# First queries and keys by two plain transfers each, values requested before the placing, the second pair's rounding one step later

## The chip, the cores and the metric

The kernel runs on one core of one Trainium2 chip. The core has five engines with an instruction queue each: TensorE (PE; its weight loads are shown as PEld), VectorE (DVE), ScalarE (ACT), GpSimd (POOL) and SyncE (SP), which here issues every DMA. Sixteen DMA engines carry the transfers. The metric is the device time of one execution in microseconds (us); of a kernel the median of its runs is given.

## What is computed

Attention that keeps, for every query, the scores that reach the 32nd largest, then two feed-forward blocks. Cut to what matters (B, H, S, D = 4, 8, 576, 64):

```
scores = scale * q @ k.T                      # per batch and head, 576 x 576
kth = 32nd largest of each row
attn = softmax(where(scores >= kth, scores, -1e9)) @ v
x = attn of all heads, side by side           # 2304 x 512
x = soft mixture of 8 experts on 32 slots (phi, w1, w2)
out = (g of x @ w_in) @ w_out                 # g(h) = h * tanh(softplus(h))
```

## The kernel before

Attention comes first. Heads are taken in 16 pairs (four batches of four). The 1152 queries of a pair are nine tiles of 128; two tiles make a step, so attention has 72 steps, numbered m. Steps -2 and -1 only produce scores. Within `run` (L415) the list `ORDER` fixes by hand in which order the pieces of a step are written, and every engine executes its own instructions in that order.

One step of one pair of tiles goes like this. TensorE makes scores (L223) from operands that are kept as sums of a rounded and a low part: `Qs` holds rounded queries above their low parts, `Ka` the rounded keys twice, `Kb` the low parts of the keys and the row of maxima. ScalarE copies the scores, four copies of 288 columns a step, into a tile `x` (L433). VectorE folds `x` (h L238, f L239 and L240) and finds the 32nd largest value by rounds of eight maxima (L260, L264, L267); GpSimd adds two operations to the fold (f L246, L250). In step -1 VectorE does GpSimd's part (L242). Then ScalarE makes a mask `R` (L280) and exponentials (L321), and TensorE multiplies with the values (L326). Scores and copies are made two steps ahead of the maxima, the fold one step ahead. The tile h has one buffer.

Loading has three layers. Pair i needs queries and keys with the heads on 128 partitions (`load`, L153, into `rawq` and `rawk`, one buffer each), their rounding on ScalarE (`split_hi`, L158), the low parts (`split_lo`, L161: VectorE for pair 0, GpSimd for the others), and copies inside SBUF which put the parts of each head into `Qs`, `Ka` and `Kb` (`place`, L173, five transfers a head, and `place_b`, L176). `load_v` (L191) brings `vT` and the values `V` in five transfers; `phi` comes in two.

The very first head has a way of its own, `first_head` (L178): it loads 64 rows of queries and 64 rows of keys, each onto both halves of the partitions, into a tile `E`, rounds them on ScalarE straight into place (L185, L186), and VectorE writes the rest (L187 to L189). No placing is needed. The second head of pair 0 goes by `load` and `place`. Twelve matmuls on zeros (L147) warm TensorE up meanwhile.

For the later pairs `prepare` (L569) puts each of these pieces at a step, `LEAD` steps from the pair's first; the function `at` (L427) moves what would be due earlier to step -1, or to -2 for loads. Only pair 1 (first step 4) is touched by that limit: its roundings and the low part of its queries were put at step -1, and the placing of its first head.

Weight fetches for the experts are written between the steps of attention. Experts and the last block follow.

Of the kernel before, what the change touches and what calls it, by code (L numbers as in the profile page):

```python
# [23 lines left out]
B, H, S, D = 4, 8, 576, 64  # L24
# [65 lines left out]
class Attention:  # L90
# [87 lines left out]
    def first_head(self):  # L178

        nc = self.nc  # L180
        raw = self.w2.tile([128, 2, 576], F32, name="E")
        for n, name in enumerate("qk"):
            nc.sync.dma_start(raw[:, n], self.io[name + "T"][0, 0, None, 0:64].to_broadcast([2, 64, 576]))
        hi = self.w2.tile([128, 576], F32R, name="V")
        nc.scalar.copy(hi, raw[:, 0])  # L185
        nc.scalar.copy(self.Ka[0], raw[:, 1])  # L186
        nc.vector.tensor_copy(self.Qs[0][0:64, :576], hi[0:64].bitcast(F32))  # L187
        nc.vector.tensor_tensor(self.Qs[0][64:128, :576], raw[64:128, 0], hi[64:128].bitcast(F32), op=ALU.subtract)
        nc.vector.tensor_tensor(self.Kb[0][0:64], raw[0:64, 1], self.Ka[0][0:64].bitcast(F32), op=ALU.subtract)  # L189
# [225 lines left out]
    def run(self, between=None):  # L415
        nc = self.nc
# [5 lines left out]
        todo, carry, sides = collections.defaultdict(list), {}, dict(x=([], []), y=([], []))  # L422
# [2 lines left out]
                ended[n // 2] = i, GROUPS[t]  # L425

        def at(m, token, f):  # L427
            todo[max(m, -2 if token == "Z" else -1)].append((token, f))

        def copy(m, ps, u, hf):  # L430
            if m not in X:
# [39 lines left out]
        def side(name, m, engine):  # L471

            wait, now = sides[name]
            if not now and wait and wait[0][0] <= m:
                g = wait.pop(0)[1]
                now += [g, next(g)]
            if now and engine in (now[1], None):
                now[1] = next(now[0], "")
                if not now[1]:
                    now.clear()  # L480

        def step(m):
# [39 lines left out]
            if m - 2 in ended:  # L522

                iv, gv = ended[m - 2]
                for slot in IN_GROUP[gv[4]]:
                    add("v", lambda slot=slot: values(exs[m - 2][0], iv, gv, slot))
                if gv[1][-1] in (4, 8):

                    key, rs, rc = (iv, gv[0]), [], []
                    at(m + 1, "s", lambda: rs.append(self.sums(avs[key], key[1], m > M)))  # L530
                    at(m + 1, "i", lambda: rc.append(self.recip(rs[0])))
                    if m > M:
                        at(m + 1, "i", lambda: self.last_logits(avs[key], rc[0], iv))
                    for t in range(5):
                        at(m + 1, "n", lambda t=t: self.normalize(avs[key], rc[0], xls[key[0]], key[1], t))
                    at(m + 2, "l", lambda: ending(*key))
# [32 lines left out]
        def prepare(j):  # L569

            first = 9 * j // 2
            d = Ds[j] = {}
            for n in "qk":
                at(first + LEAD[0], "Z", lambda n=n: self.load(d, j, n))
            for q, n in enumerate("qk"):
                at(first + LEAD[1] + q, "H", lambda n=n: self.split_hi(d, n))
                at(first + LEAD[2] + q, "L", lambda n=n: self.split_lo(d, n, nc.gpsimd))
            for h in range(2):
                for n in "qk":
                    at(first + LEAD[3] + h, "D", lambda h=h, n=n: self.place(d, j, h, n))  # L580
            at(first + LEAD[4], "D", lambda: self.load_v(d, j))
            for h in range(2):
                at(first + LEAD[6 + h], "D", lambda h=h: self.place_b(j, h))
            sides["y"][0].append((first + LEAD[5], self.fold_phi(d, j)))

        with self.tc.manual_schedule(engines={ENG.Activation, ENG.PE, ENG.DVE, ENG.Pool, ENG.SP}):
            d = Ds[0] = {}
            self.first_head()
            for n in "qk":
                self.load(d, 0, n)  # L590
            for n in "qk":
                self.split_hi(d, n)
                self.split_lo(d, n, nc.vector)
                self.place(d, 0, 1, n)
            pv = self.io["phi"].rearrange("(p h d) s -> h d p s", h=2, d=D)
            for h in range(2):
                nc.sync.dma_start(self.phi[64 * h : 64 * h + 64, :, 32 * h : 32 * h + 32], pv[h])
            self.load_v(d, 0)
            sides["y"][0].append((0, self.fold_phi(d, 0)))
            for h in range(2):  # L600
                self.place_b(0, h)
            for j in range(1, npairs):
                prepare(j)
            for m in range(-2, M + 4):
                step(m)
            n = iter(IDLE)

            def warm():
                for _ in range(next(n)):
                    nc.tensor.matmul(idle[:, :256], self.k.idn.bitcast(BF16)[:, :128], self.k.idn.bitcast(BF16), start=True, stop=True)  # L610

            while sum(sides["x"], []):
                if sides["x"][1] and sides["x"][1][1] == "P":
                    warm()
                side("x", M, None)
            warm()
# [439 lines left out]
```

## Time and profile before

| | us |
|---|---|
| median of 3 runs | 855.86 |
| the runs | 850.24 to 857.74 |
| the profiled execution | 856.29 |
| its span, from the first to the last instruction | 854.4 |
| TensorE busy | 762.4 (89%) |
| VectorE busy | 742.8 (87%) |
| ScalarE busy | 592.0 (69%) |
| GpSimd busy | 414.5 (49%) |
| mean granted TensorE clock | 0.953 of full speed |

All times in rows are microseconds from the span's start. A row of a timeline gives the start, the length, the engine, the line, the operation, what is written and read, and in brackets how long the engine had been idle and what ended that. SPq is the queue of SyncE; its rows give how long the issue of a transfer took, not the transfer. A clock of 1.00 is the full 2.4 GHz, 0.50 the lower level, 1.2 GHz.

### The profile page before, as it was taken

The numbers are of one execution on the slowest core, as the hardware profiler recorded it, in microseconds if no ns is written. First come the engines' busy times: TensorE is split into PE (matmuls) and PEld (weight loads), VectorE is DVE, ScalarE is ACT, GpSimd is POOL, SyncE is SP. The second block draws the span as 40 slices with busy tenths as digits, with TensorE's granted clock in tenths as the row PEclk, the third lists the DMA queues.
The fourth block names the chain that finished last, engine by engine and source line by source line (L and its number), as shares of the span: only waits on it lengthen the run. The fifth ranks groups of instructions, "written<-read, shape, count | busy, mean of one in ns | idle before, by whom it ended". The sixth has DMA issues, their size and how long they took to land.

```text
span 854.4 us, 17813 instructions
## 1 busy us (share of the span) xinstructions
PE 762.4 (89%) x6222; PEld 657.3 (77%) x6222; DVE 742.8 (87%) x2206; ACT 592.0 (69%) x1330; POOL 414.5 (49%) x475
## 2 busy tenths in 40 slices
PE   4689999999999999999999998885378889999997
PEld 2578898898888899888988886653366677888885
DVE  3999999997997999999999936869989999869673
ACT  3478888886887888989888743328664755766462
POOL 3466576565665556666665610003444544443332
PEclk7699999998998999999999999996789999999999
DMA  3636545643653755465344478990220001001011
GB/s 83 162 78 168 127 122 151 169 116 95 168 135 86 208 130 152 119 168 126 70 106 126 157 289 330 399 371 9 90 99 0 1 37 38 1 0 74 1 38 42
DMA packets 60984, 103.41 MB, mean 121 GB/s; under 512 B 24852, under 2 KB 24852, under 8 KB 59860
## 3 DMA queue, kind: packets, MB, share of 16 engines
q1 hardware_dynamic: 60884, 102.18, 40.9%
q8 instruction: 51, 0.84, 0.4%
q14 instruction: 49, 0.40, 0.1%
HBM read 69.86 MB, written 4.72 MB: 87 GB/s over the span
## 4 chain that ended last, share of the span: by engine, by line
PE 45%; DVE 30%; ACT 12%; DMA 5%; issue 4%; SPq 2%; POOL 1%; DVEq 0%; POOLq 0%; ACTq 0%
PE av L326 8%; PE o L975 6%; PE o L974 6%; PE o L976 6%; DVE f L264 5%; ACT R L280 4%; DVE m L267 4%; DVE m L260 4%; DVE h L238 3%; PE st L320 3%; PE st L315 3%; PE s L223 2%; DVE e L940 2%; PE st L316 2%; ACT x L433 2%
## 5 line engine op out<-in xcount | busy, mean ns | idle before, releaser
L326 PE MATMUL av<-V,E 112*107 112x97 f32 (+5 forms) x1600 | 192.3, 268 | 1.6 <-ACT E L321 1.6
L326 PEld LDWEIGHTS av<-V,E 112*107 112x107 f32 (+5 forms) x1600 | 178.6, 183 | 1.8 <-ACT E L321 1.7
L246 POOL TENSOR_TENSOR f<-x,h 128x576 int32<-128x576 int32 x71 | 100.5, 1415 | 139.9 <-DVE f L240 62.8
L1010 ACT ACTIVATE e<-e 128x768 f32<-128x768 f32 (+2 forms) x168 | 115.4, 744 | 76.2 <-DVE e L940 75.8
L321 ACT ACTIVATE E<-st 128x320 f32<-128x320 f32 (+2 forms) x256 | 117.4, 488 | 60.1 <-PE st L320 57.3
L950 POOL TENSOR_TENSOR gl<-hs,gh 128x768 fp32r<-128x768 f32 (+2 forms) x56 | 92.3, 1648 | 131.0 <-DVE gh L949 124.6
L264 DVE MATCH_REPLACE8 f<-m,f 128x100 f32<-128x100 f32 (+2 forms) x432 | 131.4, 311 | 0.0
L223 PE MATMUL s<-Ka,Qs 128*128 128x288 f32 x320 | 104.9, 341 | 19.7 <-ACT x L433 10.1
L260 DVE MAX8 m<-f 128x8 f32<-128x100 f32 (+2 forms) x432 | 118.4, 315 | 0.0
L975 PE MATMUL o<-w,gl 128*128 128x512 f32 x288 | 116.9, 406 | 0.7 <-POOL gl L950 0.7
L974 PE MATMUL o<-w,gh 128*128 128x512 f32 x288 | 116.7, 405 | 0.0
L976 PE MATMUL o<-w,gh 128*128 128x512 f32 x288 | 115.9, 402 | 0.0
L280 ACT ACTIVATE R<-x,m 128x576 bf16<-128x576 f32 x142 | 112.0, 796 | 1.6
L315 PE MATMUL st<-Qs,Ka 128*128 128x256 f32 (+1 forms) x320 | 110.3, 352 | 2.3 <-ACT E L321 1.5
L433 ACT COPY x<-s 128x288 f32<-128x288 f32 x288 | 101.9, 409 | 8.3 <-PE s L223 7.3
L250 POOL TENSOR_TENSOR f<-f,x 128x576 int32<-128x576 int32 x71 | 100.5, 1416 | 0.6
L267 DVE MAX8 m<-f 128x8 f32<-128x576 f32 x144 | 100.8, 741 | 0.0
L316 PE MATMUL st<-Qb,Kb 128*128 128x256 f32 (+1 forms) x320 | 94.0, 303 | 4.3 <-ACT Qb L305 4.3
L223 PE MATMUL s<-Kb,Qs 96*128 96x288 f32 x320 | 93.7, 307 | 0.3 <-DVE Kb L189 0.3
L320 PE MATMUL st<-dm,R 128*128 128x128 bf16 (+1 forms) x790 | 88.9, 219 | 4.9 <-ACT R L280 4.1
L223 PEld LDWEIGHTS s<-Ka,Qs 128*128 128x128 f32 x320 | 63.3, 198 | 22.9 <-ACT x L433 11.6
L938 DVE COPY hs<-h 128x768 f32<-128x768 f32 (+2 forms) x56 | 46.9, 838 | 30.6 <-PE h L936 30.4
(152 smaller groups left out, 1438.7 us busy)
## 6 DMA issues: line engine op xcount, KB each, us to landing
w<-in_w SPq DMA_DIRECT2D x30, 1024.0 KB, 7.6
Ka<-hik SPq DMA_DIRECT2D x62, 144.0 KB, 2.6
raw<-in_w_in SPq DMA_DIRECT2D x8, 1024.0 KB, 8.4
raw<-in_w_out SPq DMA_DIRECT2D x8, 1024.0 KB, 5.2
rawq<-in_qT SPq DMA_DIRECT2D x16, 288.0 KB, 3.5
rawk<-in_kT SPq DMA_DIRECT2D x16, 288.0 KB, 3.6
vT<-in_vT SPq DMA_DIRECT2D x16, 288.0 KB, 3.7
Qb<-Qs SPq DMA_DIRECT2D x32, 144.0 KB, 2.6
```

The costliest lines, as they stand in the source:

```text
L223: nc.tensor.matmul(ps, q, k, start=n == 0, stop=n == len(todo) - 1)
L260: V.max(M[j][u], f[:, u, part])
L264: V.match_replace(out=f[:, u, part], in_to_replace=M[j][u], in_values=f[:, u, part], imm_value=NEG)
L267: V.max(M[3][u], f[:, u])
L280: self.nc.scalar.activation(R, x, AF.Relu, bias=m8[:, t, 31:32], scale=-1.0)
L315: T.matmul(ps[:, j], self.Ka[z][:, ks], self.Qs[z][:, 64 * h + q0 : 64 * h + q0 + n], start=j == 0, stop=False, skip_group_check=True)
L321: return lambda: nc.scalar.activation(ex[:, cs[0] : cs[0] + len(cs), :n], ps, AF.Exp, scale=SCALE)
L326: self.nc.tensor.matmul(av[:w, j], ex[:k, c, o : o + w], V[:k, c, h], start=c == 0 and j == 2 * h, stop=c == 4, skip_group_check=True)
L433: nc.scalar.copy(X[m][:, u, 288 * hf : 288 * hf + 288], ps)
L974: T.matmul(ps, gh[:, c, r : r + 128], w[0], start=f == 0, stop=False)
L975: T.matmul(ps, gl[:, c, r : r + 128], w[0], start=False, stop=False)
L976: T.matmul(ps, gh[:, c, r : r + 128], w[1], start=False, stop=f == 15)
```

## The change

Three edits, all at the beginning of attention.

In `first_head` each of the two loads, which had a source repeated twice (`[2, 64, 576]`), becomes two plain transfers of 64 partitions.

In `at` the limit is step 0 instead of step -1, except for loads.

At the top of `run`'s program, the transfers of `phi` and `load_v` of pair 0 are written ahead of the rounding and placing of its second head, not behind.

```
 # first_head
-            nc.sync.dma_start(raw[:, n], self.io[name + "T"][0, 0, None, 0:64].to_broadcast([2, 64, 576]))
+            for r in (0, 64):
+                nc.sync.dma_start(raw[r : r + 64, n], self.io[name + "T"][0, 0, 0:64])
 # run, at
-            todo[max(m, -2 if token == "Z" else -1)].append((token, f))
+            todo[max(m, -2 if token == "Z" else 0)].append((token, f))
 # run
             self.first_head()
             for n in "qk":
                 self.load(d, 0, n)
+            pv = self.io["phi"].rearrange("(p h d) s -> h d p s", h=2, d=D)
+            for h in range(2):
+                nc.sync.dma_start(self.phi[64 * h : 64 * h + 64, :, 32 * h : 32 * h + 32], pv[h])
+            self.load_v(d, 0)
             for n in "qk":
                 self.split_hi(d, n)
                 self.split_lo(d, n, nc.vector)
                 self.place(d, 0, 1, n)
-            pv = self.io["phi"].rearrange("(p h d) s -> h d p s", h=2, d=D)
-            for h in range(2):
-                nc.sync.dma_start(self.phi[64 * h : 64 * h + 64, :, 32 * h : 32 * h + 32], pv[h])
-            self.load_v(d, 0)
             sides["y"][0].append((0, self.fold_phi(d, 0)))
```

SyncE, from its first transfer on, before (line numbers move by one behind the first edit):

```order
L183 DMA E<-in_qT 128x1x576
L183 DMA E<-in_kT 128x1x576
L153 DMA rawq<-in_qT 128x576
L153 DMA rawk<-in_kT 128x576
L173 DMA Qs_117<-hiq 64x576
L173 DMA Qs_117<-rawq 64x576
L173 DMA Ka_118<-hik 64x576 x2
L173 DMA Kb_119<-rawk 64x576
L597 DMA phi<-in_phi 64x4x32 x2
L195 DMA vT<-in_vT 128x576
L200 DMA V<-in_v 112x4x64
L201 DMA V<-in_v 128x64
```

and now:

```order
L184 DMA E<-in_qT 64x576 x2
L184 DMA E<-in_kT 64x576 x2
L153 DMA rawq<-in_qT 128x576
L153 DMA rawk<-in_kT 128x576
L594 DMA phi<-in_phi 64x4x32 x2
L196 DMA vT<-in_vT 128x576
L201 DMA V<-in_v 112x4x64
L202 DMA V<-in_v 128x64
L201 DMA V<-in_v 112x4x64
L202 DMA V<-in_v 128x64
L173 DMA Qs_117<-hiq 64x576
L173 DMA Qs_117<-rawq 64x576
```

The first two loads have become four, and the placing of the second head (L173) has moved behind phi, vT and the four pieces of V; what follows behind is as before.

ScalarE from its first instruction on, with the semaphores that each row waits for (DMAHW0 to DMAHW7 are counted up by landed transfers, PE, DVE and Pool by the engines), before:

```order
L185 ACT_TABLE_LOAD
L185 CAST V<-E 128x576 [waits DMAHW0_49]
L186 CAST Ka_121<-E 128x576 [waits DMAHW1_49]
L158 CAST hiq<-rawq 128x576 [waits DMAHW2_49]
L158 CAST hik<-rawk 128x576 [waits DMAHW3_49]
L433 COPY x<-s 128x288 [waits PE_49] x4
L433 COPY x<-s 128x288 [waits PE_49,Pool_49]
L433 COPY x<-s 128x288 [waits PE_49] x3
L158 CAST hiq<-rawq 128x576 [waits DMAHW4_49,DMAHW2_49,DVE_49]
L158 CAST hik<-rawk 128x576 [waits DMAHW6_49,DMAHW7_49,DMAHW3_49,DVE_49]
L433 COPY x<-s 128x288 [waits PE_49,Pool_49]
L433 COPY x<-s 128x288 [waits PE_49] x3
```

and now:

```order
L186 ACT_TABLE_LOAD [waits DMAHW1_49]
L186 CAST V<-E 128x576 [waits DMAHW0_49]
L187 CAST Ka_121<-E 128x576 [waits DMAHW3_49,DMAHW2_49]
L158 CAST hiq<-rawq 128x576 [waits DMAHW4_49]
L158 CAST hik<-rawk 128x576 [waits DMAHW5_49]
L434 COPY x<-s 128x288 [waits PE_49] x4
L434 COPY x<-s 128x288 [waits PE_49,Pool_49]
L434 COPY x<-s 128x288 [waits PE_49] x3
L434 COPY x<-s 128x288 [waits PE_49,Pool_49]
L434 COPY x<-s 128x288 [waits PE_49] x3
L158 CAST hiq<-rawq 128x576 [waits DMAHW5_49,DMAHW4_49,DVE_49]
L158 CAST hik<-rawk 128x576 [waits DMAHW5_49,DMAHW7_49,DMAHW0_49,DVE_49]
```

The second pair's roundings (the second hiq and hik) now stand behind four more copies, those of step 2's scores; the wait for the second transfer of queries (DMAHW1) stands ahead of the table load, which waited for nothing.

GpSimd, behind its first memsets, in the steps -1 to 1, before:

```order
L161 TENSOR_TENSOR rawq<-rawq,hiq 128x576
L246 TENSOR_TENSOR f<-x,h 128x2x288
L291 TENSOR_SCALAR mx<-col 128x2
L292 TENSOR_TENSOR mx<-col,mx 128x2
L250 TENSOR_TENSOR f<-f,x 128x2x288
L161 TENSOR_TENSOR rawk<-rawk,hik 128x576
```

and now:

```order
L247 TENSOR_TENSOR f<-x,h 128x2x288
L292 TENSOR_SCALAR mx<-col 128x2
L293 TENSOR_TENSOR mx<-col,mx 128x2
L251 TENSOR_TENSOR f<-f,x 128x2x288
L161 TENSOR_TENSOR rawq<-rawq,hiq 128x576
L161 TENSOR_TENSOR rawk<-rawk,hik 128x576
```

The low part of the second pair's queries has moved from ahead of the fold's two operations to behind them. On TensorE and VectorE no instruction has moved.

## Rows read from the trace of the kernel before

**Rows 1.** Chain of waits, first 100 us: start, length, what the end waited for
```profile
1.52 14.22 DMA E<-in_kT
...
26.32 4.32 DMA rawk<-in_kT
...
34.99 1.56 DVE f L239
...
74.08 0.34 ACT xl L345
```

**Rows 2.** Stretches: from:to, length, busy us (instructions) by engine, TensorE clock, DMA share, GB/s
```profile
5.00:5.50 0.50, 0.50 (x3) 0.18 (x2) 0.00 (x0) 0.00 (x0) 0.50 (x2) 1.00 0.13 51
...
7.50:8.00 0.50, 0.00 (x0) 0.00 (x0) 0.00 (x0) 0.00 (x0) 0.39 (x3) 1.00 1.04 378
...
9.50:10.00 0.50, 0.00 (x0) 0.00 (x0) 0.00 (x0) 0.06 (x1) 0.00 (x0) 1.00 0.13 51
...
75.00:150.00 75.00, 72.58 (x662) 66.89 (x661) 73.91 (x290) 64.47 (x176) 49.51 (x65) 1.00 0.55 144
...
520.00:550.00 30.00, 25.00 (x529) 18.81 (x517) 25.58 (x53) 10.20 (x20) 0.62 (x5) 1.00 1.03 404
```

**Rows 3.** Timeline of SyncE's queue at the start: start, length of the issue
```profile
2.10 4.07 SPq L153 DMA_DIRECT2D rawq<-in_qT  x1
...
19.87 0.52 SPq L173 DMA_DIRECT2D Kb<-rawk  x1
20.43 1.36 SPq L597 DMA_DIRECT2D phi<-in_phi  x2
21.84 0.60 SPq L195 DMA_DIRECT2D vT<-in_vT  x1
22.48 0.43 SPq L200 DMA_DIRECT2D V<-in_v  x1
```

**Rows 4.** DMA issues, whole run: count, KB each, median us from issue to landing
```profile
rawq<-in_qT SPq DMA_DIRECT2D x16, 288.0 KB, 3.5
...
Qs<-rawq SPq DMA_DIRECT2D x31, 144.0 KB, 2.4
...
phi<-in_phi SPq DMA_DIRECT2D x2, 32.0 KB, 2.2
```

**Rows 5.** Timeline of ScalarE, first 33 us
```profile
0.73 1.28 ACT L185 ACT_TABLE_LOAD   x1 [0.73 <-PEq L1050]
...
9.95 0.67 ACT L185 CAST V<-E 128x576 fp32r<-128x576 f32 x1 [7.93 <-DMA E<-in_qT]
...
28.97 0.67 ACT L158 CAST hiq<-rawq 128x576 fp32r<-128x576 f32 x1 [7.23 <-DMA rawq<-in_qT]
...
31.29 0.99 ACT L433 COPY x<-s 128x288 f32<-128x288 f32 x3
```

**Rows 6.** Timeline of VectorE, first 42 us
```profile
11.13 0.76 DVE L188 TENSOR_TENSOR Qs<-E,V 64x576 fp32r<-64x576 f32 x1
...
19.86 0.76 DVE L238 TENSOR_TENSOR h<-x 128x576 f32<-128x576 f32 x1 [1.17 <-ACT x L433]
...
25.22 0.75 DVE L238 TENSOR_TENSOR h<-x 128x576 f32<-128x576 f32 x1
...
26.00 0.46 DVE L239 TENSOR_TENSOR f<-h 128x288 f32<-128x288 f32 x1
...
33.12 1.84 DVE L238 TENSOR_TENSOR h<-x 128x576 f32<-128x576 f32 x1 [1.75 <-ACT x L433]
...
41.32 0.75 DVE L238 TENSOR_TENSOR h<-x 128x576 f32<-128x576 f32 x1
```

**Rows 7.** Timelines of TensorE and GpSimd, first 37 us
```profile
17.37 0.58 PE L223 MATMUL s<-Kb,Qs 96*128 96x288 f32 x1 [0.27 <-DVE Kb L189]
...
31.14 1.41 POOL L246 TENSOR_TENSOR f<-x,h 128x576 int32<-128x576 int32 x1
...
34.30 1.93 POOL L161 TENSOR_TENSOR rawk<-rawk,hik 128x576 f32<-128x576 f32 x1
```

## The prediction

> **What bounds the kernel now.** I read the chain of waits of the first 100 us, then the stretches of the first 16 us, then each engine's timeline there. The reader should see that the start is a wait for one transfer. The chain begins with the second of the two broadcast transfers, issued at 1.52 us and 14.22 us long [rows 1]. While it flows, 13% of the 16 DMA engines are busy, which is two engines, and move 51 GB/s; in the half microsecond in which the two 128-partition loads flow beside it, the engines move 378 GB/s [rows 2]. So the first queries reach ScalarE at 9.95 us [rows 5], and VectorE starts its first tile (the maximum h, here called h(0)) at 19.86 [rows 6]. The rest of the first 42 us holds a second loss: h(1) is at 25.22, h(2) at 33.12 after 1.75 us of idling for ScalarE, h(3) at 41.32 [rows 6]. From there the chain stays on VectorE until 74.08 [rows 1], so what VectorE gains before 41 us should move everything behind it. Later the work is a loop over engines: in 75 to 150 us TensorE is busy 72.58 and VectorE 73.91 of 75 us [rows 2].
>
> **First term: the loads.** Each broadcast becomes two plain transfers of 64 partitions; SP has two issues more. An issue of such a transfer takes 0.52 to 0.60 us [rows 3], and the program's second one starts at 1.52 [rows 1]. So the four are issued at 0.7, 1.52, 2.1 and 2.7, rawq at 3.3 and rawk at 3.9. The 4.07 us that the issue of rawq took [rows 3] stood behind the two busy engines, and I expect it gone. From issue to landing: no row shows a plain 64-partition load of this size from HBM. The bounds are 2.2 us (phi, 64 partitions, from HBM) below and 3.5 (rawq, twice the size) above; the same shape inside SBUF takes 2.4 [rows 4]. The worst single one is 4.32, rawk in the chain [rows 1]. I take 2.8: queries landed at 1.52 + 2.8 = 4.3, keys at 2.7 + 2.8 = 5.5.
>
> The order shows a new wait here that the diff doesn't. A rounding of the queries now has two transfers to wait for, and the wait for the second half stands ahead of the table load on ScalarE. Before, that load ran from 0.73 for 1.28 us under the wait for data [rows 5] and cost nothing; now its cover is gone, and it runs from 4.3 to 5.6. Then: queries rounded 0.67 [rows 5], 5.6 to 6.25; the two Qs writes on VectorE, which before ended 1.27 after that rounding (11.13 + 0.76 against 9.95 + 0.67) [rows 5, 6], until 7.5; keys rounded by 6.95, since they landed at 5.5; Kb 0.76 more, until 8.25; the first matmul with Kb 0.15 later, as before (17.37 [rows 7]), at 8.4. rawq (landed at 6.8) and rawk (7.4) are rounded until 8.3, while ScalarE has nothing else, and VectorE takes their low parts (0.76 each) until 9.8.
>
> TensorE's clock: the warm-up matmuls run until 7 us and the clock is still granted in full, 1.00 (the 2.4 GHz level), in 9.5 to 10 us with TensorE idle since [rows 2]; before, the first scores ran at the lower level and it took 2.5 us from the first Kb matmul to h(0) (17.37 [rows 7], 19.86 [rows 6]). Now the gap is half a microsecond, so I take the full clock: 0.5 for the first pair of matmuls and four copies at 0.33 (0.99 for three [rows 5]), h(0) at 8.4 + 1.8 = 10.2. At the lower level it would be 10.9. The term is 19.86 - 10.2 = **9.7 us**. Bounds: landing after 2.2 us gives 10.3; landing after 4.32 and the lower level, 7.4.
>
> The Trainium skill speaks against one price here: ScalarE: Activation LUTs, What ACT_TABLE_LOAD costs, gives 2.66 us for a switch, with a drain of 1.38 behind the 1.28. The row shows 1.28. By the Trainium skill h(0) would come 1.4 us later and the time would be 845.4.
>
> **Second term: the second pair's rounding.** Before, ScalarE idled 7.23 us for rawq of the second pair, until 28.97 [rows 5], with the last four copies for h(2) queued behind. rawq was late since SP issued it behind the placing, phi and the values; h(2) lost 1.75 us [rows 6]. Taking this wait away alone would win little: GpSimd's f L246 stood behind the low part of rawq, as the order shows, and ended at 31.14 + 1.41 = 32.55 [rows 7], and h(2) overwrites the one buffer that it reads. That is why the order on GpSimd matters: now both f operations come first. The four copies stand ahead of the roundings on ScalarE, too.
>
> Are the inputs there? SP now issues phi, vT and four pieces of V from 4.5 to 8.5 (1.36 + 0.60, and 0.43 and a little more for each piece of V [rows 3]), which costs the placing nothing, since the low part of rawq is ready only at 9.0. Five placings take until 11.5, and Kb lands near 14. The scores for h(2) and their copies follow in 2 to 3 us, at 17, and h(2) is due at 10.2 + 5.36 (25.22 - 19.86) + 6.15 (33.12 - 1.75 - 25.22) = 21.7. Cover: over 4 us. The raw loads of the second pair are issued near 13 and 14 and land by 18.3. ScalarE stands there for rawk until then, but the next copies are due only at h(3), and the first mask (R) needs the last maxima of step 0, which VectorE finishes behind h(1).
>
> What is late next is the port: before, h(2) took 1.84 instead of 0.75 and the f operation after it 1.56 instead of 0.46 [rows 1, 6], 2.2 us together, while GpSimd ran L250 and the low part of rawk, itself 1.93, where L246 of the same shape took 1.41 [rows 7]. Now GpSimd runs L246 from 17.1 (behind VectorE's L240), the maxima, L250 until 20.5, rawq until 21.9 and rawk behind it. h(2) at 21.7 meets the end of the one and the f operation the whole of the other: about 1.3 us, with 0 and 2.2 as bounds. The term is 1.75 + 2.2 - 1.3 = **2.6 us**; bounds 1.75 and 3.9. h(3) would be at 21.7 + 6.0 (41.32 - 33.12 - 2.2) + 1.3 = 29.0, against 41.32.
>
> The second pair's operands: rawk's low part ends near 23.8 and is placed by 27; TensorE first needs it close to h(3). Nothing on the path. Instructions on VectorE and TensorE are the same in number and order.
>
> **Sum.** 9.7 + 2.6 = 12.3 us. The profiled execution took 856.29 (span 854.4), so 844.0. The median of the runs shown is 855.86, 0.4 lower; the runs lie 850.24 to 857.74 apart, and about 1% (8.6 us) is what a measurement here can tell from no change.
>
> **Rivals.**
> - *Forecast, both terms pass through: 844.0.* For it: weight fetches, route and experts are put at steps of the attention, so they move with it. Chance 0.55; with the bounds of the terms alone, 842.1 to 847.1.
> - *The second term is lost.* ScalarE, held until 28.97, was behind VectorE, and TensorE with it; if they, and not h(2) and h(3), set the beat from there on, only the common shift of 9.7 stays: 846.6. Against it: the chain runs on VectorE without a break until 74. With a late landing beside it, 847 to 849. Chance 0.24.
> - *The gain is given back at the weights.* In 520 to 550 us the DMA engines are full (share 1.03, 404 GB/s [rows 2]). If that stretch ended when it does whatever the attention did, up to all 12.3 would be lost: 850 to 856. Against it: the loads there are issued from step 68 on and wait for buffers of the attention. Chance 0.13.
> - *The halves bring nothing.* If two halves still went one after the other at today's 51 GB/s, keys would land near 15.8 again, and the bare second term less the table load's 1.28 is left: about 855. A rule of the Trainium skill points that way: DMA: Bandwidth & Descriptors, Rules for kernel authors, says not to bother with two transfers to disjoint partition halves, since they serialize. The trace bears out only that they share engines: at 378 GB/s a half is 147 KB, 0.4 us, less than its issue, and what it replaces runs on two engines. Chance 0.05.
> - *Slower than before.* Placing stands behind six more loads, with many small packets. If these held the engines, Kb of the second head would land late and TensorE, in order, with it. At 14 us it has over 4 us of cover; above 18.5 each microsecond is lost, and above some 31 the kernel is slower than before. The six loads would have to take 17 us more than they did, where each landed in 2 to 4. At 24 us more: about 863. Chance 0.03.
>
> **Numbers.** Faster by over 1% (under 847.3): the first case and nearly all of the second, 0.77. Within 1%: the rest of it and the next two, 0.20. Slower: 0.03. The range 840 to 850 takes the bounds of both terms (842.1 to 847.1), the second rival, and some of the spread of the runs shown.
>
> **What would show it.** The table load at about 4.3 instead of 0.73; first rounding at 5.6; first Kb matmul at 8.4, on a full clock; h(0) at 10.2, h(2) without a wait for ScalarE at 21.7, h(3) near 29; GpSimd's low parts behind L250; no idle time of 7 us on ScalarE. Behind 75 us every row of before some 12 us earlier. Wrong would be: queries or keys landing after 6 us; a wait of TensorE for Kb that reaches h(2); or h(3) on time but the later stretches less than 10 us earlier.

## The result, and the profile after

The changed kernel takes 845.7 us (median of six runs, 840.73 to 850.1) against 856.72 for the kernel before in the same comparison: ratio 0.9881, 95% interval 0.9832 to 0.9931. In a second comparison it took 849.39 against 855.96, ratio 0.9884 (0.9824 to 0.9945). Predicted were 844.0, a range of 840 to 850, and "faster by over 1%" with 0.77. The kernel is faster; whether by over 1% the interval leaves open, and it holds the forecast (844.0) as well as the second rival's 846.6. The profiled execution took 850.1, span 848.2, and was the longest of its six; what follows therefore compares places in the trace first and times second.

I follow the change by the maxima h(i), one a step, and call "lead" how much earlier a row stands than in the kernel before. Line numbers are one higher than before.

ScalarE's timeline, first 19 us (start, length, engine, line, operation, count, in brackets the idle time ahead and what ended it); it answers to [rows 5]:

```profile
4.25 1.28 ACT L186 ACT_TABLE_LOAD   x1 [4.25 <-DMA E<-in_qT]
5.54 0.67 ACT L186 CAST V<-E 128x576 fp32r<-128x576 f32 x1
6.12 0.67 ACT L187 CAST Ka<-E 128x576 fp32r<-128x576 f32 x1
7.70 0.67 ACT L158 CAST hiq<-rawq 128x576 fp32r<-128x576 f32 x1 [0.92 <-DMA rawq<-in_qT]
8.56 0.67 ACT L158 CAST hik<-rawk 128x576 fp32r<-128x576 f32 x1 [0.19 <-DMA rawk<-in_kT]
9.14 0.99 ACT L434 COPY x<-s 128x288 f32<-128x288 f32 x3
...
17.54 0.67 ACT L158 CAST hiq<-rawq 128x576 fp32r<-128x576 f32 x1
```

The idle 7.93 and 7.23 us of before are gone. VectorE's timeline, which answers to [rows 6]:

```profile
10.90 0.76 DVE L239 TENSOR_TENSOR h<-x 128x576 f32<-128x576 f32 x1 [0.88 <-ACT x L434]
...
22.34 0.95 DVE L239 TENSOR_TENSOR h<-x 128x576 f32<-128x576 f32 x1
23.32 1.56 DVE L240 TENSOR_TENSOR f<-h 128x288 f32<-128x288 f32 x1
...
29.65 0.74 DVE L239 TENSOR_TENSOR h<-x 128x576 f32<-128x576 f32 x1
...
55.66 1.26 DVE L239 TENSOR_TENSOR h<-x 128x576 f32<-128x576 f32 x1
```

The last row is h(7), 66.08 in the kernel before. h(0) leads by 8.96, h(3) by 11.67 (41.32 - 29.65). The lead stays 11.68 until h(6), is 10.42 at h(7), 10.08 at h(8) and 9.15 from h(11) to h(28). At h(29) it rises by 2.0, at h(42) it falls by 2.9; h(71) leads by 8.32 and the span is 6.2 shorter.

The chain of waits of the first 75 us (start, length, what the end waited for) shows where the first loss sits; [rows 1] had VectorE there without a break:

```profile
3.90 4.64 DMA rawk<-in_kT
8.56 0.67 ACT hik L158
...
9.59 0.86 PE s L224 x2
...
10.90 0.77 DVE h L239
...
33.32 0.43 PE m L302 x3
...
55.47 0.96 PE av L327 x10
...
64.48 0.49 SPq L202
65.02 2.66 DMA V<-in_v
```

From 33.32 us on the chain runs on TensorE, until 64.30, and behind it waits for values that SyncE could request only late. Why TensorE was late stands in two views, its timeline around 30 us and the stretches from 8 us on (busy us by PE, PEld, DVE, ACT, POOL, each with its count, then granted clock, DMA share, GB/s):

```profile
29.17 0.29 PE L224 MATMUL s<-Kb,Qs 96*128 96x288 f32 x1
33.32 0.43 PE L302 MATMUL m<-idr,mx 128*2 128x128 f32 x3 [3.85 <-POOL mx L293]
...
33.95 0.44 PE L224 MATMUL s<-Kb,Qs 96*128 96x288 f32 x1
```

```profile
8.00:10.00 2.00, 1.38 (x7) 1.12 (x8) 1.75 (x3) 1.81 (x5) 0.67 (x2) 0.78 0.85 220
10.00:12.00 2.00, 2.00 (x10) 2.00 (x9) 1.09 (x3) 1.42 (x5) 0.00 (x0) 0.50 0.96 232
...
30.00:32.00 2.00, 0.00 (x0) 0.00 (x0) 1.97 (x5) 0.04 (x1) 0.58 (x1) 1.00 0.97 244
32.00:34.00 2.00, 0.68 (x5) 0.68 (x6) 2.00 (x13) 0.95 (x2) 1.92 (x4) 0.76 0.79 151
34.00:36.00 2.00, 2.00 (x12) 1.80 (x11) 2.00 (x10) 1.86 (x5) 0.69 (x2) 0.50 0.66 254
...
40.00:42.00 2.00, 2.00 (x13) 1.60 (x12) 2.00 (x10) 1.43 (x3) 0.73 (x1) 0.50 0.01 4
42.00:44.00 2.00, 2.00 (x17) 2.00 (x16) 1.97 (x5) 1.71 (x4) 0.46 (x1) 0.68 0.40 93
```

TensorE was idle for 3.85 us, waiting for GpSimd's maxima of step 2; then the clock is granted at 0.50, the 1.2 GHz level, until about 43, with TensorE busy all the time. The Kb matmul of 288 columns, 0.29 long at 29.17, takes 0.44 at 33.95. TensorE's work of two steps falls behind, though VectorE came on time to h(6).

### The profile page after: what moved, and what is told of

It reads as the page before. It is cut to its first block, busy times and chain, and to the rows that moved or that the text cites. A ratio compares the mean times of both kernels' runs of the same rounds, so it can differ in the third digit from the quotient of the medians.

```text
span 848.2 us, 17819 instructions
## 1 busy us (share of the span) xinstructions
PE 767.8 (91%) x6222; PEld 662.1 (78%) x6222; DVE 743.8 (88%) x2206; ACT 593.5 (70%) x1330; POOL 415.3 (49%) x475
## 4 chain that ended last, share of the span: by engine, by line
PE 47%; DVE 27%; ACT 10%; DMA 8%; issue 4%; SPq 2%; POOL 1%; DVEq 0%; POOLq 0%; ACTq 0%
PE av L327 10%; PE o L975 6%; PE o L977 6%; PE o L976 6%; DVE f L265 4%; PE s L224 4%; DVE m L261 3%; DVE m L268 3%; PE st L316 3%; PE st L321 3%; ACT R L281 3%; PE st L317 3%; DMA w<-in_w 2%; DVE h L239 2%; DVE e L941 2%
```

## The experiments

Two theories on the size of the gain. A: the two terms reach VectorE as worked out, and what is lost behind h(6) is lost to TensorE at its lower clock. B: the second term was never worth anything in the time (TensorE and ScalarE set the beat), and the loads are all of it. A third question is what moves the lead by 2 to 5 us at h(29), h(34), h(38) and h(42). The kernel before took a median of 853.78 to 855.96 in the four comparisons that follow.

### The loads alone, and all but the loads

`loads_only` undoes the second and third edit, `no_loads` the first (the edits against the kernel before, cut):

```
 # loads_only
+            for r in (0, 64):
+                nc.sync.dma_start(raw[r : r + 64, n], self.io[name + "T"][0, 0, 0:64])
 # no_loads
-            todo[max(m, -2 if token == "Z" else -1)].append((token, f))
+            todo[max(m, -2 if token == "Z" else 0)].append((token, f))
 (and phi and load_v ahead of the placing)
```

> Only the plain loads of the first head; roundings, placing and values as before. My theory (the loads are the first term, and the late roundings a separate second one): first Kb matmul at 8.4 us and h(0) at 10.9, as in the changed kernel; ScalarE again idle, for rawq of the second pair, until about 20; h(2) at about 24 with a wait of 1.5 to 2 us, h(3) at about 32.2 where the changed kernel has 29.65. Time about 9 us under the kernel before, 848. Rival (all three edits are one gain, the loads alone are taken back by the next wait): h(3) later than 35 and a time within 4 us of before.

> The changed kernel with the two broadcast loads of before. My theory: keys land at 15.8 and h(0) is at 19.9 as before; the roundings no longer hold up h(2), which comes at 31.4, and h(3) at 38.6 (2.7 us sooner than before). Time 2 to 3 us under before, about 854. Rival (roundings and order are worth nothing alone): h(3) at 41.3 and no difference.

`loads_only`: 844.96 us, ratio 0.9871 (0.9818 to 0.9924). h(0) at 10.29, lead 9.57; h(2) at 24.27, h(3) at 32.77, lead 8.55; h(13) 7.43. Its timelines of ScalarE and VectorE:

```profile
20.66 0.67 ACT L158 CAST hiq<-rawq 128x576 fp32r<-128x576 f32 x1 [8.59 <-DVE m L261]
```

```profile
24.27 0.76 DVE L239 TENSOR_TENSOR h<-x 128x576 f32<-128x576 f32 x1 [2.47 <-POOL f L247]
25.07 1.71 DVE L240 TENSOR_TENSOR f<-h 128x288 f32<-128x288 f32 x1
```

The stall on the second pair's rounding stays when the loads alone are made faster, 8.59 us on ScalarE now (the row puts its end down to VectorE; the transfer of rawq, issued at 16.66 us and landed after 3.9, ended at the same time), and VectorE waits 2.47 us for GpSimd's fold, which stands behind the low part of rawq. That is the order on GpSimd which the prediction spoke of.

`no_loads`: 854.64 us, ratio 1.0001 (0.9969 to 1.0034). Both roundings of the second pair run without a wait for data (hiq at 25.89), h(2) comes at 30.75, 2.37 earlier, h(3) at 38.05, lead 3.27, h(13) 2.95. So the second term is there in the trace, 3.27 - 0.54 (its lead at h(0)) = 2.73, and it is not to be seen in the time: the interval reaches 2.7 us to either side. For the loads, mechanism and time agree as far as the interval, some 4.5 us to either side, can tell. A holds for the trace; for the time, B is not refuted here.

### Each of the later edits left out

`no_round` keeps the limit of -1, `no_order` keeps phi and the values behind the placing:

```
 # no_round
-            todo[max(m, -2 if token == "Z" else 0)].append((token, f))
+            todo[max(m, -2 if token == "Z" else -1)].append((token, f))
 # no_order: phi, load_v
+            for n in "qk": split_hi, split_lo, place
             phi
             self.load_v(d, 0)
-            for n in "qk": split_hi, split_lo, place
```

> The changed kernel with the limit of step -1 as before: second pair's roundings ahead of the four copies, its low part of queries ahead of the fold on GpSimd. Theory: with values requested ahead, rawq and rawk of the second pair land by 18 us, so the roundings end at about 18.8 and the copies at 20, ahead of h(2) at 22.3; h(3) within 0.5 us of 29.65, the time that of the changed kernel within 2 us. Rival (the step of the rounding is what the second term came from): h(2) waits 1 us or more, h(3) at 31 or later.

> The changed kernel with placing ahead of phi and values as before: plain loads and later rounding alone. The loads alone left h(2) at 24.27 and h(3) at 32.77; with values ahead but the old rounding step h(3) was at 29.35. Theory (rounding step and request order each suffice to free h(2)): h(2) at 22.0 to 22.4, h(3) 29 to 30. Rival (only the request order does): h(2) later than 23.5, h(3) later than 31.

`no_round`: 845.89 us, ratio 0.9888 (0.9841 to 0.9934). h(3) at 29.35, lead 11.97, and the lead is still 12.00 at h(13). `no_order`, one execution: 841.48; h(3) at 30.04, lead 11.28, h(13) 10.20. ScalarE's timelines, first of `no_round`, then of `no_order`:

```profile
16.23 0.67 ACT L158 CAST hiq<-rawq 128x576 fp32r<-128x576 f32 x1 [3.74 <-DMA rawq<-in_qT]
```

```profile
21.11 0.67 ACT L158 CAST hiq<-rawq 128x576 fp32r<-128x576 f32 x1 [4.13 <-DMA rawq<-in_qT]
```

Either edit does the work of the other. With the values ahead of the placing, rawq of the second pair lands early enough for a rounding in step -1 (h(2) at 23.25, without a wait). With the rounding a step later, ScalarE's 4.13 us lie behind the copies, and h(2) comes at 21.71, also without a wait. With both, h(3) came at 29.2 to 29.7 in four executions, no earlier than without the second edit (29.35 in `no_round`, 29.01 and 29.31 in `small_no_round` and `best` below).

### The table load, and the two halves

`early_table` gives ScalarE a copy of one column ahead of everything, so that the table load has nothing to wait for. `one_load` replaces the two halves of each first load by one plain transfer of 128 partitions; its lower half brings rows of the second head, so part of the first head is computed from them.

```
 # early_table
+        nc.scalar.copy(self.c.tile([128, 1], F32, name="one"), self.k.eps)
 # one_load
-            for r in (0, 64):
-                nc.sync.dma_start(raw[r : r + 64, n], self.io[name + "T"][0, 0, 0:64])
+            nc.sync.dma_start(raw[:, n], self.io[name + "T"][0, 0])
```

> The changed kernel with one more copy on ScalarE, of 128x1, ahead of the roundings, so that the table load stands under no wait for data. By the prediction's step, which charged the table load 1.28 us, the first Kb matmul comes at 7.1 and h(0) at 9.6 or sooner. Rival (something else is late at the same time: the copies of scores stand on ScalarE behind the rounding of the second head's keys, which land at 8.6): Kb matmul at 7.1, but the first copy not before 9.1 and h(0) at 10.5 to 10.9, so that the new wait costs nothing.

> The changed kernel with one plain transfer of 128 partitions for the first queries and one for the keys in place of two of 64 each; the lower half of the partitions then gets the second head's rows, so the low parts of the first head are wrong, all work is the same. Theory (a transfer costs its issue, 0.6 us, and the halves flow at full rate): two issues less, keys and both raw loads land 1.2 us sooner, first copy at about 8 and h(0) at 9.4 to 9.9. Rival (halves serialise beyond their issues): more than 2 us sooner; rival (issue is hidden): no difference.

ScalarE's timeline in `early_table`, then in `one_load`:

```profile
0.74 1.28 ACT L182 ACT_TABLE_LOAD   x1 [0.74 <-PEq L1052]
...
4.31 0.67 ACT L187 CAST V<-E 128x576 fp32r<-128x576 f32 x1 [2.08 <-DMA E<-in_qT]
6.24 0.67 ACT L188 CAST Ka<-E 128x576 fp32r<-128x576 f32 x1 [1.26 <-DMA E<-in_kT]
...
8.36 2.79 ACT L435 COPY x<-s 128x288 f32<-128x288 f32 x8
```

```profile
0.74 1.28 ACT L185 ACT_TABLE_LOAD   x1 [0.74 <-PEq L1050]
3.60 0.67 ACT L185 CAST V<-E 128x576 fp32r<-128x576 f32 x1 [1.58 <-DMA E<-in_qT]
4.55 0.67 ACT L186 CAST Ka<-E 128x576 fp32r<-128x576 f32 x1 [0.28 <-DMA E<-in_kT]
...
7.98 2.80 ACT L433 COPY x<-s 128x288 f32<-128x288 f32 x8
```

Without the wait the queries are rounded 1.23 us earlier (4.31 against 5.54), but the keys only at 6.24, when they land, and the first Kb matmul gains 0.57 (7.84 against 8.41). That is neither the 1.28 us which the prediction charged for the table load nor the rival's nothing. h(0) comes at 9.81, 1.09 or 0.70 earlier than in the two executions of the changed kernel (10.90, 10.51). Against the first, 0.57 of it is the earlier Kb matmul; the rest comes with copies that run without a gap, on a TensorE whose clock is still 1.00 until 12 us. `one_load` has h(0) at 9.44, the largest lead at h(3) (13.16) and at h(13) (12.82). In seven executions whose program is the changed kernel's up to there, h(0) came at 10.36 to 10.90. So the halves with the wait that they bring cost 0.9 to 1.5 us against one transfer, by a single execution of it, and the broadcast cost 9. The times of these single executions, 848.24 and 845.96, say nothing of it: they hold the later waits, for which see below.

### The lower clock behind step 2

`after_again` repeats the changed kernel. `bridge` adds 30 matmuls on constants to it, where TensorE waits ahead of step 3's maxima rows.

```
+        def fill(n):
+            ps = self.pS.tile([128, 288], F32, name="s")
+            for _ in range(n):
+                nc.tensor.matmul(ps[:, :256], self.k.idn.bitcast(BF16)[:, :128], self.k.idn.bitcast(BF16), start=True, stop=True)
-                add("p", lambda: pms.append(self.maxima_rows(g, mxs.pop(m - 1))))
+                add("p", lambda: (fill(30) if m == 3 else None, pms.append(self.maxima_rows(g, mxs.pop(m - 1)))))
```

> The changed kernel again, for a second profile. What is fixed by the program should recur: h(0) 10.9, h(3) 29.65, the low granted clock in 33 to 43 us, the step of 7.8 us at h(7). What is chance should not: the 2.9 us that the profiled execution lost at 282 to 292 us against the kernel before. If both recur at the same place, the second is the program's too. Time 845 plus or minus 4.

> The changed kernel, and 30 matmuls on a constant on TensorE (results unused) just ahead of step 3's row of maxima, where it idled from 29.9 to 33.3 us. Theory (the granted clock fell because TensorE ran out of work there, and the low level in 33 to 43 us is what cost VectorE 1.6 us at h(7) and h(8) and 0.9 at h(11)): clock 1.00 through 30 to 45 us, step from h(6) to h(7) 6.5 instead of 7.3 to 7.8, h(13) some 12 us sooner than in the kernel before instead of 9.2 to 10.2. Rival (the loss at h(7) comes from the values or operands of the second pair, late by the step): clock kept, but h(7) still over 7 us behind h(6).

`after_again` lost its lead in the same places: 12.12 until h(6), 11.40 at h(7), 10.18 from h(11). The loss at 282 to 292 us recurred too, 2.89 at h(42) where the first had 2.91; by what was said ahead of this run that makes it the program's, see the next part. `bridge`: 843.28 us (four runs, 841.03 to 853.89), ratio 0.986 (0.9827 to 0.9894, without the longest run), which the time alone can't tell from the changed kernel's 0.9881 and 0.9884. TensorE's timeline in it, one of its stretches, and h(7):

```profile
29.30 3.45 PE L486 MATMUL s<-idn 128*128 128x256 bf16 x30
33.28 0.31 PE L302 MATMUL m<-idr,mx 128*2 128x128 f32 x3 [0.53 <-POOL mx L293]
```

```profile
34.00:36.00 2.00, 2.00 (x20) 1.90 (x19) 2.00 (x10) 1.98 (x6) 0.67 (x2) 1.00 0.58 225
```

```profile
54.33 1.26 DVE L239 TENSOR_TENSOR h<-x 128x576 f32<-128x576 f32 x1
```

In 34 to 36 us TensorE carries out 20 matmuls, where the changed kernel had 12. The maxima's matmul starts where it did (33.28, 33.32), the clock is 1.00 throughout from 28 to 46 us, and the lead is 11.72 at h(3), 11.75 at h(7) and 11.41 at h(13). The step from h(6) to h(7) is 6.52, where the changed kernel had 7.80 and 7.26. The program differs in nothing else, so the lower clock is shown to cost the changed kernel 1.6 to 2.2 us here (2.52 and 1.93 lost in its two executions, 0.31 with the filling matmuls).

Over all kernels with the new loads in which h(2) is on time, the length of the lower stretch between 28 and 46 us and the lead lost between h(3) and h(13) go together in the main. The length is worked out from the clock in stretches of 2 us, 4 x (1 - share) each:

| kernel | lower clock, us | lead at h(3) | lost by h(13) |
|---|---|---|---|
| changed | 10.2 | 11.67 | 2.52 |
| small_fetch (below) | 10.2 | 11.94 | 2.55 |
| after_again | 10.2 | 12.11 | 1.93 |
| early_table | 10.2 | 12.80 | 1.81 |
| no_order | 6.8 | 11.28 | 1.08 |
| small_no_round (below) | 6.8 | 12.31 | 1.08 |
| one_load | 6.8 | 13.16 | 0.34 |
| no_round | 3.4 | 11.97 | none |
| bridge | 0 | 11.72 | 0.31 |
| best (below) | 0 | 12.01 | none |

Length is not all: `one_load` has 6.8 too, but over by 36 us, and loses only 0.34, where in `no_order` and `small_no_round` it lasts until 41.

Of the 2.52, 1.26 are TensorE's lateness at h(7). The 0.34 at h(8) are not the clock's: the operation h(7) is 1.26 long in `bridge` too, at full clock, and 1.25 to 1.27 in every kernel with the second edit, 0.92 or 0.93 in every kernel without it, so they come with that edit (GpSimd's low part of rawk runs beside it, until 54.98 in `bridge`, 54.40 in `no_round`, where h(7) is at 54.33 and 54.09). The other 0.93 at h(11) is the transfer of V in the chain above, whose request follows TensorE's matmuls there.

The kernel before has this loss in some executions as well. In `small_before` (below), which does the same work up to there, the clock is 0.50 from 46 to 52 us, where the profiled execution of the kernel before had 1.00, and h(11) comes 1.12 later.

### The waits behind 180 us

The lead of h(29) changed by +2.0 in the changed kernel, -1.0 in its repeat and +4.6 in `no_round` and `loads_only`, which do the same work there. The chains of waits between 170 and 300 us have transfers of operands as their longest links; first the kernel before, then the changed one:

```profile
189.85 7.98 DMA vT<-in_vT
...
246.73 6.41 DMA Ka<-hik
```

```profile
175.72 4.09 DMA Kb<-rawk
...
180.69 7.60 DMA vT<-in_vT
...
234.92 7.34 DMA Qs<-rawq
...
270.17 7.12 DMA vT<-in_vT
```

SyncE issues a weight fetch of 1 MB at 180.21, 206.34, 233.05, 263.84 and 282.70 us; three of them stand less than 7 us ahead of such a link. The last link is the loss at h(42); the repeat has it too (vT at 271.84, 7.09 long), `bridge`, `no_round` and `loads_only` lose nothing there. So it depends on when the request falls, and whether the shorter executions of the changed kernel have it is not shown. `small_fetch` is the changed kernel with the weight fetches in pieces of half the size, at twice as many places; `small_before` is the kernel before with the same; `small_no_round` the first with the limit of -1; `best` has the filling matmuls too.

```
-            for n in range(2 * NUNIT):
-                between[8 + 4 * n].append(lambda u=n // 2, c=n % 2: fetch(u, [c]))
+            for n in range(4 * NUNIT):
+                between[8 + 2 * n].append(lambda u=n // 4, c=n % 4: fetch(u, [c], 4))
```

> The changed kernel, with each weight fetch of the attention in quarter pieces of half the size, at every second place of the order instead of every fourth. Theory that the late waits come from operand transfers which queue behind a whole weight piece: the transfers of 7 to 8 us in the chain of waits near 180, 235 and 270 us shrink to 5 us or less, the steps h(29), h(38) and h(42) lose their 2 to 3 us, attention ends 13 to 18 us earlier than before instead of 6.5 to 8.3, median 837 to 842. Rival, that the DMA engines have the same bytes in the queue whatever the pieces: the same waits, median 844 to 849. The first 100 us as in the changed kernel by either: h(3) near 29.4, h(13) 9 to 10 earlier than before.

> The changed kernel with three additions: the limit of -1 for the second pair's rounding is kept as before the change, 30 matmuls on constants (256 columns) stand on TensorE ahead of step 3's maxima rows, and the weight fetches come in quarter pieces. Theory: h(3) near 29.4, no loss at h(7), h(8), h(11), h(13) 12 us earlier than before (92.3), and the late waits shortened as in the run with quarter pieces alone, so a median of 834 to 840. Rival, the pieces make no difference: h(13) at 92.3 too, but a median of 841 to 845, as without them.

> The kernel before the change, with the weight fetches of the attention in quarter pieces: the change is undone, the steadier transfers are kept. Two sums stand against each other. If the change is worth what its first 13 steps show (9.2 and 10.2 us in two executions of the changed kernel, 9.4 with quarter pieces), the median here is 9 to 10 above the changed kernel with quarter pieces, 848 to 849, and the pieces are worth about 6 us to either kernel. If the whole change were worth what the prediction's sum had, 12.3, it would be 851; if the loss behind attention were real and only 6 us arrived, 845. The first 13 steps as in the kernel before: h(0) near 19.9, h(13) near 104.3.

> The changed kernel without its second edit (the limit of -1 is kept), with the weight fetches in quarter pieces. If the second edit costs the low clock behind step 2, as one execution without it showed, h(13) is again near 92.3 (12.0 earlier than before) and the median 836 to 837, 2 to 3 below the 838.9 of the changed kernel with quarter pieces. Rival, that execution had the full clock by chance: h(7), h(8) and h(11) lose 2.6 us here too, h(13) near 94.9, median 839.

| kernel | us | runs | ratio to before (95%) | lead h(3) | h(13) | h(71) |
|---|---|---|---|---|---|---|
| small_before | 850.27 | 848.52 to 851.46 | 0.995 (0.9933 to 0.9967) | 0.11 | -0.97 | 7.58 |
| small_fetch | 838.91 | 838.6 to 839.87 | 0.9823 (0.9802 to 0.9844) | 11.94 | 9.39 | 18.86 |
| small_no_round | 838.04 | 836.38 to 838.72 | 0.9812 (0.9775 to 0.9849) | 12.31 | 11.23 | 20.33 |
| best | 837.82 | 835.43 to 841.03 | 0.9818 (0.9781 to 0.9855) | 12.01 | 12.02 | 21.14 |

The DMA issues between 170 and 300 us (count, KB each, median us to landing), of the changed kernel and of `small_fetch`:

```profile
w<-in_w SPq DMA_DIRECT2D x5, 1024.0 KB, 6.4
...
vT<-in_vT SPq DMA_DIRECT2D x4, 288.0 KB, 6.7
```

```profile
w<-in_w SPq DMA_DIRECT2D x10, 512.0 KB, 4.9
...
vT<-in_vT SPq DMA_DIRECT2D x5, 288.0 KB, 4.9
```

With smaller pieces vT lands after 4.9 instead of 6.7, the chain between 170 and 300 us of `small_fetch` has no transfer in it, h(29) and h(38) gain 4.8 and 5.0 us on the kernel before (4.8 and 4.0 in `small_before`), and the runs of `small_fetch` lie 1.3 us apart, those of the changed kernel 9.4. So the late waits are those for operands behind a large weight piece. That they are also what scatters the runs is likely but not shown: `small_no_round` scatters by 2.3 us and `small_before` by 2.9, but `best`, with the same small pieces, by 5.6. `best` gained 2.6 at h(13) over `small_fetch` and 1.1 in the time; the three fastest kernels can't be told apart, and their runs (835.43 to 841.03) lie below nearly all of the changed kernel's (840.73 to 852.89).

Against this steadier background the change itself is worth 850.27 - 838.91 = 11.4 us (by the ratios, 0.995 - 0.9823 of 854.5, 10.9; the two were measured in different comparisons, and their intervals together allow some 2.3 us to either side). That is more than the 9 to 10 that the first 13 steps let expect, and does not exclude them: `small_before` has a wait of its own for V at h(11), 1.1 us, behind its lower clock, so at h(13) the two stand 10.36 apart, and 11.28 at h(71). For `small_no_round` the rival was half right: the lower clock is there from 34 to 41 us, h(7) and h(8) lose nothing, h(11) loses 1.09.

## Why the prediction was right

**The new wait ahead of the table load** was read from the order, and was right to a tenth: the load at 4.25 (4.3 predicted), the queries' rounding at 5.54 (5.6), Kb at 7.51, the first Kb matmul at 8.41 (8.4). E landed in a median of 2.8 and 2.9 us, where 2.8 had been chosen between 2.2 and 3.5. What the wait costs was put too high, though: without it, in `early_table`, the Kb matmul gained 0.57 and not 1.28, since the keys' landing came next. No second part of the table load showed: the rounding begins 0.01 behind it. The Trainium skill, ScalarE: Activation LUTs, What ACT_TABLE_LOAD costs, has a drain of 1.38 us for a switch; here nothing had run on the engine before, and the row does not show it. By the Trainium skill the rounding would have come at about 6.9 (an estimate, 5.54 and the drain).

**The first term** was 8.96 instead of 9.7, inside its bounds. What was mis-sized is the landing of rawq and rawk: 3.5 us was taken from a median over the whole run, rawk took 4.64 (the chain above). Its rounding at 8.56 stood ahead of the first copies, which began at 9.14, TensorE waited, and in 8 to 10 us the clock is at 0.78, from 10 on at 0.50. h(0) then came 2.49 behind the Kb matmul, which is the 2.49 of before at the lower level; 10.9 had been named for it. The full clock that the sum had taken held in the repeat: 1.00 until 14 us, no wait for rawk, and h(0) 1.87 behind the Kb matmul (8.64, 10.51), where 1.8 had been summed; its term is 9.35. In `early_table`, at full clock too, it came 1.97 behind.

**The second term** was 2.71 (11.67 - 8.96) against 2.6: no wait at h(2), and of the 2.2 us at the port (the time that VectorE's operations took longer beside GpSimd's) h(2) kept 0.2 and the f operation 1.1 (1.56 instead of 0.46), the 1.3 that had been taken. GpSimd's order and the cover for Kb (TensorE waited 0.19 us for it at 14.20) were as worked out. What the prediction did not see is that two edits each do this alone.

**The step that failed** is the sentence that what VectorE gains before 41 us moves everything behind it. 2.5 us of 11.7 were lost between h(6) and h(11), all but 0.34 of them to TensorE, the place of the rival which forecast 846.6; the measured 845.7 lies between it and the forecast. The rival's reason was half right. The second term was not lost at h(3), and no steady beat of TensorE took it; the 3.85 us without work around 30 us let the clock fall, and the work behind it ran at the lower level. In the kernel before the lower level lasted until about 37 us too, but TensorE's dense work began only at 32, inside the stall that the change removes:

```profile
34.00:36.00 2.00, 1.98 (x10) 1.66 (x10) 1.97 (x2) 1.14 (x3) 2.00 (x2) 0.50 0.24 51
36.00:38.00 2.00, 2.00 (x14) 1.96 (x14) 2.00 (x4) 1.95 (x5) 1.17 (x2) 0.61 0.33 68
```

The prediction read the clock only where the first scores run, in 9.5 to 10 us [rows 2]. With smaller weight pieces about 11 us arrive, give or take 2.3, where 12.3 had been summed.

That the time came so near the forecast is in part luck. The two profiled executions lead by 9.15 and 10.18 at h(13) and, behind the late waits, by 8.32 and 6.56 at h(71), with spans only 6.2 and 4.1 us shorter; they are among the longest of their runs, which lie 9.4 and 9.9 us apart. The medians, 10.2 us apart by the ratio, happen to fall near a sum that had neither TensorE's loss nor these waits.

**The rivals.** *The gain is given back at the weights*: no; with smaller pieces the lead of h(71) over `small_before` is 11.28 and the spans differ by 12.3 (849.1, 836.8). In the pair as given the weights took nothing either: of the 8.32 at h(71), 8.48 stand behind the stretch of full DMA engines (ScalarE's mh, 573.77 and 565.29 us) and 7.91 at VectorE's last copy (848.37, 840.46); the difference to the spans' 6.2 lies behind that copy. In the profiled execution of the changed kernel a part was given back at h(42), to a transfer behind a fetch (vT, 7.12 in the chain), while `bridge`, the same work there, lost nothing at h(42). *The halves bring nothing*: no; the Trainium skill, DMA: Bandwidth & Descriptors, Rules for kernel authors, advises against two halves, and the trace agrees only in part: `one_load` is 0.9 to 1.5 us earlier at h(0), while the broadcast that they replace cost 9. *Slower*: no; the placing waited for nothing long.

**What stays open.** Whether the second and third edit are worth anything in the time: `loads_only`, `no_round` and the changed kernel lie at 844.96, 845.89 and 845.7 to 849.39, inside each other's intervals, and `loads_only` was not run with smaller weight pieces. At h(71) its one profile leads by 13.50, the changed kernel's two by 8.32 and 6.56. The second edit in particular brings nothing at h(3) that the third does not, costs the 0.34 at h(8), and the lower stretches of 10.2 us are all in kernels that have it; `small_no_round` leads `small_fetch` by 1.84 at h(13), but their times (838.04, 838.91) are not apart. Why the lower stretch is 10.2 us in some kernels and 3.4 or 6.8 in others is open. The idle time ahead of it does not settle it: 3.85 (changed), 3.81 (`one_load`, 6.8), 2.49 (`no_round`, 3.4), 1.87 (`small_no_round`, 6.8), and at 45 us 1.76 in the kernel before, with none, and 1.52 in `small_before`, with 6.8.

## What to carry to other kernels

A transfer that keeps two of sixteen DMA engines busy at the very start holds up everything behind it: without it the keys were rounded 9.65 us sooner (15.77, 6.12), and 8.96 of that reached h(0). The order after such a change has to be read for waits that moved (here a table load behind a landing). A gain on the engine that sets the end is safe only as far as the others have work at full clock: look for stretches in which TensorE will now run dry ahead of a dense part. And where medians of like kernels scatter by 4 us, compare places in the trace, and look for large transfers ahead of small ones that someone waits for; cutting them in two gave 4.5 us in the kernel before (854.78 to 850.27) and narrowed the interval of the changed kernel's ratio from 0.010 to 0.004, though to 0.007 only in `small_no_round` and `best`.

## What the runs showed of the hardware that was not expected

An idle time of 3.85 us on TensorE was followed by about 10 us at the 1.2 GHz level with the engine busy throughout, and filling that gap with matmuls on constants kept 1.00. In `one_load` plain loads of 128 partitions by 576 took 0.40 to 0.43 us to issue, less than the halves of 64 partitions in the changed kernel (0.57 to 0.60), so two halves cost SyncE three times the issue time of the whole: 1.22 against 0.40. Behind the halves the whole ones took 0.59 and 0.43.
